# Expert layers with a token-major second layer, the gate folded into the rows, the next rows transposed inside the branch, and an early job of 256 rows

## The chip, the cores and the metric

The kernel runs on one core of a Trainium2 chip. The metric is the device time of one execution, in microseconds. TensorE (PE in the profile, its weight loads PEld) does the matmuls and transposes into PSUM, VectorE (DVE) and ScalarE (ACT) work on PSUM and SBUF, GpSimd (POOL) does some elementwise work and issues the indirect DMAs, SyncE (SP) issues the plain loads.

## The reference

What is computed is a retention layer over 4 batches, 8 heads, 768 positions and 64 channels, and then a mixture of 8 experts in which each of the 3072 tokens goes to one expert:

```python
for t in range(S):
    state = gamma[None, :, None, None] * state + np.einsum('bhd,bhe->bhde', k[:, :, t], v[:, :, t])
    y[:, :, t] = scale * np.einsum('bhd,bhde->bhe', q[:, :, t], state)
...
logits = x @ w_gate
expert_idx = np.argmax(logits, axis=1)
...
gate_w = probs[np.arange(N), expert_idx]
...
    h = np.maximum(x_sorted[lo:hi] @ w1[e], 0.0)
    y_sorted[lo:hi] = h @ w2[e]
...
return (gate_w[:, None] * y).astype(np.float32)
```

Here x is 3072 x 512, w1[e] is 512 x 1024, w2[e] is 1024 x 512, everything in float32.

## The kernel before

**Retention.** The sequence is cut into 6 chunks of 128 positions. A step is one chunk c of one batch b, 24 steps in all, c outer. Step n loads q, k and v (`load`, four steps ahead, on SP), scales and transposes them (`scale_and_transpose`, one step ahead), makes scores and the output row block (`retain`), and a step later the gate logits (`logits`). After the fourth batch of a chunk, `place` finds each token's expert and its rank among that expert's tokens, adds (tile, row) of the tokens to the table `inv` by a matmul (`found`), and writes the chunk's 512 rows of x to DRAM (`x_d`), with the gate weight in an extra column.

**Routing tail.** After the last step, `cnt` counts the tokens of each expert, `arm` holds for each expert the size of its job in steps of 32 tokens, and `index` makes row numbers out of `inv`. The weights of experts 0 and 1 are loaded during retention (steps 12 and 16).

**Experts.** One job for each expert, up to 512 tokens as 4 tiles. `gather` fetches the rows of a job into `xs` (4 indirect DMAs on POOL, issued two experts ahead), `turn` transposes them on TensorE (16 transposes, evicted by DVE into `xTs`). Then a branch over the job's size (`tc.Switch`) runs `layers` on TensorE and ScalarE: layer 1 takes w1 as the stationary operand and the rows as the moving one, layer 2 takes w2 as the stationary operand and the hidden values `hT` as the moving one, so that its output `yp` is channel-major. `put` transposes it back (16 transposes, `try`), DVE multiplies by the gate weight that came along in `xs`, and 4 indirect DMAs scatter the rows to the output. In source order it is: branch of expert e, weights of e+2, `turn(e+1)`, `put(e)`, `gather(e+2)`.

The order on each engine inside retention and between branches comes from the scheduler of the tile framework, within data dependences; engines wait on semaphores, in the order of their own instructions. A matmul in float32 shows as two weight loads and two matmul rows in the trace.

## Time and profile before

| | |
|---|---|
| median of 3 runs | 737.28 us (735.62 to 745.01) |
| the profiled execution, its own time | 741.29 us |
| its span, first to last instruction | 739.5 us |
| PE matmul busy | 602.9 us (82% of the span) |
| PE weight loads busy | 411.1 us (56%) |
| DVE, ACT, POOL busy | 145.0, 91.3, 123.6 us |
| mean granted TensorE clock | 0.874 of full speed (2.4 GHz) |

The span is shorter than the execution's own time by what lies outside the first and last instruction. Busy shares are means over a retention stage, a short routing stage, eight expert stages and a tail, and these have different limits. PE is busy in most of the span, so the time is read from the stretches in which PE is idle or slow and from the work that it does in between.

### The profile page before, as it was taken

What the parts mean: (1) busy time and instruction counts of PE and PEld (TensorE: products, weight loads), DVE (VectorE), ACT (ScalarE), POOL (GpSimd) and SP (SyncE); (2) the same over time, 40 slices, a digit from 0 to 9 for tenths busy, and PEclk for the clock granted to TensorE, in tenths of its full rate; (3) what the DMA queues carried; (4) which work ended last, traced back from release to release, by engine and by line L of the source; (5) the groups of instructions that cost most, each with busy time, mean ns of one, the idle gap of its engine ahead of it and who ended that gap; (6) DMA issues with size and microseconds to landing.
All of it is one profiled execution on the core that took longest, in us unless ns stands there. A gap on an engine that the chain in (4) does not pass through costs nothing. (4 is left out here: it accounts for less than half of the span.)

```text
span 739.5 us, 7581 instructions
## 1 busy us (share of the span) xinstructions
PE 602.9 (82%) x3063; PEld 411.1 (56%) x3063; DVE 145.0 (20%) x330; ACT 91.3 (12%) x175; POOL 123.6 (17%) x159
## 2 busy tenths in 40 slices
PE   6999999998638969966995899499399679869930
PEld 5889899997625535534553454366255345535520
DVE  2554654645420010011002001100200110110020
ACT  2212222122001101100100110010011001001000
POOL 5223222221070010022003100300310220020021
PEclk9979998899858988996997899599699869969975
DMA  9949598931130340332025030403503410020010
GB/s 188 204 113 171 145 300 207 323 73 59 59 87 2 113 135 4 113 114 90 2 113 177 29 113 14 172 18 115 186 21 113 141 61 0 6 78 0 1 45 34
DMA packets 96475, 72.88 MB, mean 99 GB/s; under 512 B 77932, under 2 KB 77932, under 8 KB 96384
## 3 DMA queue, kind: packets, MB, share of 16 engines
q1 hardware_dynamic: 88096, 52.46, 26.2%
q0 software_dynamic: 5120, 12.79, 5.2%
q10 hardware_dynamic: 3168, 6.49, 2.4%
q8 instruction: 48, 0.79, 0.5%
q14 instruction: 43, 0.35, 0.2%
HBM read 61.11 MB, written 14.88 MB: 103 GB/s over the span
## 5 line engine op out<-in xcount | busy, mean ns | idle before, releaser
L395 PE MATMUL hp<-xTs,w1t 128*128 128x416 f32 (+3 forms) x512 | 190.6, 536 | 22.9 <-issue 22.9
L401 PE MATMUL yp<-hT,w2t 128*128 128x416 f32 (+3 forms) x512 | 175.0, 502 | 0.0
L395 PEld LDWEIGHTS hp<-xTs,w1t 128*128 128x128 f32 x512 | 103.6, 204 | 107.6 <-issue 86.8
L401 PEld LDWEIGHTS yp<-hT,w2t 128*128 128x128 f32 x512 | 97.3, 190 | 76.4 <-issue 52.6
L411 DVE TENSOR_SCALAR o<-try,xs 128x512 f32<-128x512 f32 x32 | 22.7, 747 | 356.2 <-PE try L409 348.9
L385 PE MATMUL trs<-ident,xs 128*128 128x128 f32 x128 | 30.7, 389 | 63.8 <-DMA xs<-x_d,at 60.0
L375 POOL DMA_INDIRECT xs<-x_d,at x32 | 32.8, 1026 | 278.0 <-DVE o L411 272.0
L397 ACT ACTIVATE hT<-hp 128x416 f32<-128x416 f32 (+3 forms) x64 | 32.5, 508 | 302.2 <-PE hp L395 302.2
L220 PE MATMUL y<-vs,am 128*128 128x64 f32 x384 | 61.0, 280 | 1.6 <-DVE am L194 0.6
L412 POOL DMA_INDIRECT out_dram<-o,at x32 | 32.1, 1003 | 177.4 <-DVE o L411 105.9
L385 PEld LDWEIGHTS trs<-ident,xs 128*128 128x128 f32 x128 | 20.4, 196 | 73.0 <-issue 59.2
L220 PEld LDWEIGHTS y<-vs,am 128*128 128x128 f32 x384 | 56.2, 207 | 4.0 <-issue 1.8
L386 DVE COPY xTs<-trs 128x512 f32<-128x512 f32 x32 | 21.9, 689 | 113.7 <-PE trs L385 113.7
L194 DVE TENSOR_TENSOR am<-sc,causal 128x512 f32<-128x512 f32 x48 | 31.4, 686 | 52.8 <-PE sc L192 52.8
L216 PE MATMUL y<-stb,qT 128*128 128x128 f32 x160 | 39.5, 331 | 0.0
L192 PE MATMUL sc<-qT,kT 64*128 64x128 f32 x384 | 37.6, 298 | 0.0
L403 ACT COPY yT<-yp 128x416 f32<-128x416 f32 (+3 forms) x32 | 15.9, 496 | 157.7 <-PE yp L401 157.7
L211 POOL COPY stb<-state 64x256 f32<-64x256 f32 x40 | 20.4, 510 | 83.7 <-DVE state L208 82.7
L192 PEld LDWEIGHTS sc<-qT,kT 64*128 64x128 f32 x384 | 29.4, 193 | 3.9 <-issue 2.7
L173 POOL TENSOR_TENSOR vs<-v,dec 128x512 f32<-128x512 f32 x24 | 25.0, 1043 | 36.5 <-PE new L201 26.2
L409 PE MATMUL try<-ident,yT 128*128 128x128 f32 x128 | 25.6, 346 | 4.3 <-DVE xTs L386 2.7
L223 ACT COPY xg<-y 128x512 f32<-128x512 f32 x24 | 14.1, 587 | 110.8 <-PE y L220 110.8
(82 smaller groups left out, 345.1 us busy)
## 6 DMA issues: line engine op xcount, KB each, us to landing
w1t<-in_moe_w_dram SPq DMA_DIRECT2D x8, 2048.0 KB, 7.8
w2t<-in_moe_w_dram SPq DMA_DIRECT2D x8, 2048.0 KB, 12.0
x_d<-xg ACTq DMA_DIRECT2D x6, 1056.0 KB, 4.8
q<-in_q_dram SPq DMA_DIRECT2D x24, 256.0 KB, 4.8
k<-in_k_dram SPq DMA_DIRECT2D x24, 256.0 KB, 4.6
v<-in_v_dram SPq DMA_DIRECT2D x24, 256.0 KB, 4.8
xs<-x_d,at POOLq DMA_INDIRECT x32, 3.5
out_dram<-o,at POOLq DMA_INDIRECT x32, 3.1
```

The lines of the kernel that those rows point to most:

```text
L173: nc.gpsimd.tensor_tensor(out=vs, in0=vt, in1=inner(gk, D), op=ALU.mult)
L192: nc.tensor.matmul(sc[j][:, a, :], lhsT=kT[r, a, :], rhs=qT[r, a, :], start=True, stop=True)
L194: nc.vector.tensor_tensor(out=am[j], in0=sc[j], in1=middle(causal[:, :], HP), op=ALU.mult)
L216: nc.tensor.matmul(y[:, ts(a, P)], lhsT=qT[:, a, :], rhs=stb[b][c % 2][:, a, :], start=True, stop=False, skip_group_check=True)
L220: nc.tensor.matmul(y[:, ts(h, D)], lhsT=am[j][:, a, :], rhs=vs[:, h, :], start=(c == 0), stop=True, skip_group_check=True)
L375: nc.gpsimd.indirect_dma_start(out=xs2[j % 2][:, t, :], out_offset=None, in_=x_d[:, :], in_offset=bass.IndirectOffsetOnAxis(ap=idx[:, t : ...
L385: nc.tensor.transpose(tr[:, dt, :], xs2[j % 2][:, t, ts(dt, P)], ident)
L395: nc.tensor.matmul(hp, lhsT=w1t[:, 0, dt, ts(f, P)], rhs=xT[:, dt, :, 0:m], start=(dt == 0), stop=(dt == DT - 1))
L397: nc.scalar.activation(out=hT[:, f, 0 : TC * m], in_=hp, func=AF.Relu)
L401: nc.tensor.matmul(yp, lhsT=w2t[:, 0, f, ts(d, P)], rhs=hT[:, f, 0 : TC * m], start=(f == 0), stop=(f == FT - 1))
L409: nc.tensor.transpose(tr[:, ts(d, P)], yT2[j % 2][:, d, t, :], ident)
L412: nc.gpsimd.indirect_dma_start(out=out[:, :], out_offset=bass.IndirectOffsetOnAxis(ap=idx[:, t : t + 1], axis=0), in_=o[:, :], in_offset=N ...
```

## The change

- Layer 2 becomes token-major (`layer2`): a tile of 128 tokens of `hT` is the stationary operand and w2, 512 columns wide, the moving one; 8 matmuls accumulate 128 x 512 outputs with the tokens on the partitions, and ScalarE copies them to `o2`. A last tile of 32 or 64 tokens is cut into 4 or 2 column parts, each with its output in other PSUM partitions; a last tile of 96 takes the full 512 columns. The 16 transposes of `put` and the DVE multiplication are gone.
- The gate weight is multiplied into the rows of x by ScalarE in `place`, ahead of the write to `x_d` (the weight is positive, so it passes through the relu). The extra column of `x_d` is gone, and `xs` is free once it is transposed.
- `turn` of the next job stands inside the branch, between the layers, evicted by ScalarE.
- After chunk 4 of 6, the first 256 tokens of expert 0 are indexed and gathered (with padding of the ranks, should there be fewer). Their two layers (`xTa`, `hTa`, `oa`) run on PE right behind the last retention step, with the routing tail interleaved between the blocks of layer 1. Expert 0's later job has only the rest.
- Scatters are declared independent of each other. The last expert scatters inside its branch. Weights of expert 0 are loaded at step 12, those of expert 1 only after retention's tiles are given up; q, k and v have 5 buffers each in place of 6.

The core of the diff:

```diff
-    OV = N // W - 1
-    ROW = DM + 16
+    EARLY = 256
...
-    x_d = dram.tile([N, ROW], F32, tag="x_d", name="x_d")
+    x_d = dram.tile([N, DM], F32, tag="x_d", name="x_d")
...
+    def turn(xs, xT, tiles, evict):
+        for t in tiles:
+            tr = ps("tr", 3, "trs").rearrange("p (a t) -> p a t", a=DT)
+            for dt in range(DT):
+                nc.tensor.transpose(tr[:, dt, :], xs[:, t, ts(dt, P)], ident)
+            evict(out=xT[:, :, ts(t, P)], in_=tr)
+
+    def layer1(n, xT, w1t, hT, f):
+        hp = ps("sc", 2, "hp")[:, 0:n]
+        for dt in range(DT):
+            nc.tensor.matmul(hp, lhsT=w1t[:, 0, dt, ts(f, P)], rhs=xT[:, dt, 0:n], start=(dt == 0),
+                             stop=(dt == DT - 1))
+        nc.scalar.activation(out=hT[:, f, 0:n], in_=hp, func=AF.Relu)
+
+    def layer2(n, hT, w2t, o, t):
+
+        m = min(n - t * P, P)
+        parts = P // m if m in (P // 4, P // 2) else 1
+        y = ps("y", 2, "ye")
+        c = DM // parts
+        for f in range(FT):
+            for j in range(parts):
+                nc.tensor.matmul(y[j * m : j * m + m, 0:c], lhsT=hT[:, f, t * P : t * P + m],
+                                 rhs=w2t[:, 0, f, ts(j, c)], start=(f == 0), stop=(f == FT - 1))
+        for j in range(parts):
+            nc.scalar.copy(out=o[0:m, t, ts(j, c)], in_=y[j * m : j * m + m, 0:c])
+
+    def scatter(o, idx, tiles):
+        for t in tiles:
+            done = nc.gpsimd.indirect_dma_start(
+                out=out[:, :], out_offset=bass.IndirectOffsetOnAxis(ap=idx[:, t : t + 1], axis=0), in_=o[:, t, :],
+                in_offset=None, bounds_check=N - 1, oob_is_err=False)
+
+            tc.declare_no_dep(done.ins, group="scatters", reason="other rows of the output")
+            tc.add_to_no_dep_group("scatters", done.ins)
...
-                t = att.tile([P, H, D], F32, tag=nm, name=nm, bufs=6)
+                t = att.tile([P, H, D], F32, tag=nm, name=nm, bufs=5)
...
+            yield
             for dt in range(DT):
                 nc.tensor.matmul(lg[:, b, :], lhsT=xT[:, dt, :], rhs=wg[:, dt, :], start=(dt == 0), stop=(dt == DT - 1))
+            yield
             if b == B - 1:
-                place(c, lg)
+                yield from place(c, lg)
...
-            gate = xg[c % 2][:, :, DM]
-            den = att.tile([P, B], F32, tag="den", name="den")
-            nc.vector.tensor_reduce(den, ex, axis=AX.X, op=ALU.add)
-            nc.vector.tensor_scalar(out=den, in0=den, scalar1=1e-9, scalar2=None, op0=ALU.add)
-            nc.vector.reciprocal(gate, den)
-            nc.scalar.dma_start(x_d[:, :].rearrange("(b c p) r -> c p b r", c=NC, p=P)[c], xg[c % 2])
...
+            x = xg[c % 2]
+            for b in range(B):
+                nc.scalar.activation(out=x[:, b, :], in_=x[:, b, :], func=AF.Copy, scale=gate[:, b : b + 1])
+            nc.scalar.dma_start(x_d[ts(c, B * P), :].rearrange("(b p) r -> p b r", p=P), x)
+            if c == NC - 2:
...
+                early.append(index(inv[:, :, 0 : EARLY // P], "_e"))
+                gather(xs2[0], early[0][0], range(EARLY // P), (c + 1) * B * P)
...
-            if n in (12, 16):
-                sets.append(weights(len(sets)))
+            if n == 12:
+                wa = weights(first, 0)
...
+        rest = logits(*done)
+        with tc.manual_schedule(engines={mybir.EngineType.PE}):
+            turn(xs2[0], xTa, range(EARLY // P), nc.vector.tensor_copy)
+            for f in range(FT):
+                layer1(EARLY, xTa, wa[0], hTa, f)
+                if f != 4:
+                    next(rest, None)
+            for _ in rest:
+                pass
+            for t in range(EARLY // P):
+                layer2(EARLY, hTa, wa[1], oa, t)
+        scatter(oa, early[0][1], range(EARLY // P))
...
+    o2 = [keep2.tile([P, TC, DM], F32, tag=f"o{i}", name=f"o{i}") for i in range(2)]
+    for t in o2:
+        nc.vector.memset(t, 0.0)
+    sets = [wa, weights(keep2, 1)]
+    cols = [(src_i[:, ts(e, TC)], dst_i[:, ts(e, TC)]) for e in range(E)]
+    HALF = EARLY // P
+
+    gather(xs2[1], cols[0][0], range(HALF, TC))
+    gather(xs2[0], cols[1][0], range(TC))
+    xT = mp.tile([P, DT, W], F32, tag="xTs", name="xTs")
+    turn(xs2[1], xT, range(HALF, TC), nc.vector.tensor_copy)
...
+    for e in range(E):
+        w1t, w2t = sets[e]
+        skip = EARLY if e == 0 else 0
+        arms = MOST - LEAST + 1 - skip // STEP
+        engines = [PE, ACT] + ([POOL] if e == E - 1 else [])
+        which = regs(e, engines)
+        if e + 1 < E:
+            xTn = mp.tile([P, DT, W], F32, tag="xTs", name="xTs")
+        hT = mp.tile([P, FT, W], F32, tag="hT", name="hT", bufs=1)
+        with tc.manual_schedule(engines={PE, ACT}):
+            for a in tc.Switch(which, arms):
+                n = STEP * (LEAST + a)
+                for f in range(FT):
+                    layer1(n, xT[:, :, skip:], w1t, hT, f)
+                if e + 1 < E:
+                    turn(xs2[e % 2], xTn, range(TC), nc.scalar.copy)
+                tiles = -(-n // P)
+                for t in [tiles - 1] + list(range(tiles - 1)):
+                    layer2(n, hT, w2t, o2[e % 2], t)
+                    if e == E - 1:
+                        scatter(o2[e % 2], cols[e][1], [t])
+        if e + 1 < E:
+            tiles = range(TC - HALF) if e == 0 else range(TC)
+            scatter(o2[e % 2], cols[e][1][:, HALF:] if e == 0 else cols[e][1], tiles)
+            xT = xTn
+        if e + 2 < E:
+            gather(xs2[(e + 1) % 2], cols[e + 2][0], range(TC))
+            sets.append(weights(first if e % 2 == 0 else keep2, e + 2))
```

**Where instructions stand, PE, end of retention.** Before, the last gate logits (`trx`, `lg`) are followed by the ranks (`rk`):

```order
L239 MATMUL lg<-wg,xT 128x8 [waits DVE_49]
L239 MATMUL lg<-wg,xT 128x8 x3
L235 MATMUL trx<-ident,xg_116 128x128 [waits Activation_49]
L235 MATMUL trx<-ident,xg_116 128x128 x3
L239 MATMUL lg<-wg,xT 128x8 [waits DVE_49]
L239 MATMUL lg<-wg,xT 128x8 x3
L263 LDWEIGHTS before [waits DVE_49]
L263 MATMUL rk<-ohs,before 128x32 [waits PE_49]
```

After, the early job's transposes (`trs` from `xs_103`) and layer 1 (`hp` from `xTa`) stand among them:

```order
L308 MATMUL lg<-wg,xT 128x8 [waits DVE_49]
L308 MATMUL lg<-wg,xT 128x8 x3
L181 MATMUL trs<-ident,xs_103 128x128 x2
L187 MATMUL hp<-xTa,w1t 128x256 [waits DVE_49]
L187 MATMUL hp<-xTa,w1t 128x256 x3
L303 MATMUL trx<-ident,xg_122 128x128 [waits Activation_49]
L303 MATMUL trx<-ident,xg_122 128x128 x3
L187 MATMUL hp<-xTa,w1t 128x256 x4
L308 MATMUL lg<-wg,xT 128x8 [waits DVE_49]
L308 MATMUL lg<-wg,xT 128x8 x3
L187 MATMUL hp<-xTa,w1t 128x256 [waits Activation_49]
```

The early job's transposes and matmuls now stand between the pieces of the routing tail on PE.

**PE, from the second layer of one expert to the next branch.** Before (the end of an arm of 512 tokens, then the code behind the branch, rows of `turn` and of `put`):

```order
L401 MATMUL yp<-hT,w2t 128x512 [waits Activation_49]
L401 MATMUL yp<-hT,w2t 128x512 x7
L517 UNCONDITIONAL_BRANCH
L385 MATMUL trs<-ident,xs_2248 128x128
L385 MATMUL trs<-ident,xs_2248 128x128 [waits DMASW6_49]
L385 MATMUL trs<-ident,xs_2248 128x128 x3
L385 MATMUL trs<-ident,xs_2248 128x128 [waits DMASW7_49,DVE_49]
L385 MATMUL trs<-ident,xs_2248 128x128 x3
L409 MATMUL try<-ident,yT_2249 128x128 [waits DVE_49] x3
L409 MATMUL try<-ident,yT_2249 128x128 x3
L409 MATMUL try<-ident,yT_2249 128x128 [waits Activation_49]
```

After (an arm of 416 tokens: the end of layer 1, the transposes of the next rows, the last tile of 32 tokens in 4 parts, the first full tile):

```order
L187 MATMUL hp<-xTs,w1t 128x416 x3
L181 MATMUL trs<-ident,xs_104 128x128 [waits DMASW0_49,PE_49]
L181 MATMUL trs<-ident,xs_104 128x128 x3
L181 MATMUL trs<-ident,xs_104 128x128 [waits DMASW1_49,PE_49]
L181 MATMUL trs<-ident,xs_104 128x128 x3
L181 MATMUL trs<-ident,xs_104 128x128 [waits DMASW3_49]
L181 MATMUL trs<-ident,xs_104 128x128 x3
L181 MATMUL trs<-ident,xs_104 128x128 [waits DMASW5_49,Activation_49]
L181 MATMUL trs<-ident,xs_104 128x128 x3
L199 MATMUL ye<-w2t,hT 32x128 [waits DMAHW3_49]
L199 MATMUL ye<-w2t,hT 32x128 x31
L199 MATMUL ye<-w2t,hT 128x512 x8
```

The transposes that wait for gathers and for evictions have moved from behind the branch to between the layers, and the code behind the branch holds none of them.

**POOL, around one expert.** Before, scatters (`out_dram`) and the gathers of the job after next (`xs`) alternate, and a scatter also waits for the scatter before it:

```order
L412 DMA out_dram<-o,at 3072x512 [waits DMASW7_49,DVE_49]
L375 DMA xs_2247<-x_d,at 128x528 [waits DMASW1_49,PE_49]
L375 DMA xs_2247<-x_d,at 128x528 [waits DMASW2_49,DVE_49]
L375 DMA xs_2247<-x_d,at 128x528 [waits DMASW3_49,DVE_49]
L412 DMA out_dram<-o,at 3072x512 [waits DMASW0_49]
L375 DMA xs_2247<-x_d,at 128x528 [waits DMASW5_49,DVE_49]
L412 DMA out_dram<-o,at 3072x512 [waits DMASW4_49]
L412 DMA out_dram<-o,at 3072x512 [waits DMASW6_49]
```

After, the gathers stand behind one scatter and wait for transposes (PE) of the expert before:

```order
L206 DMA out_dram<-o_2400,dst 3072x512 [waits DMASW4_49,Activation_49]
L151 DMA xs_103<-x_d,src 128x512 [waits DMASW5_49,PE_49]
L151 DMA xs_103<-x_d,src 128x512 [waits DMASW6_49,PE_49]
L151 DMA xs_103<-x_d,src 128x512 [waits DMASW7_49,PE_49]
L151 DMA xs_103<-x_d,src 128x512 [waits DMASW0_49,PE_49]
L206 DMA out_dram<-o_2400,dst 3072x512 [waits DMASW1_49,Activation_49]
L590 UNCONDITIONAL_BRANCH
L206 DMA out_dram<-o_2400,dst 3072x512 [waits DMASW2_49]
```

What moved is the gather: all four are issued behind one scatter, with no wait for a scatter's landing.

## Rows read from the trace of the kernel before

**Rows 1.** Stretches: us, then busy of PE, PEld, DVE, ACT, POOL, clock, DMA share, GB/s.

```profile
195.00:224.00 29.00, 8.81 (x46) 5.98 (x45) 10.18 (x36) 0.23 (x1) 15.43 (x12) 0.55 0.31 93
344.00:409.00 65.00, 53.61 (x160) 30.21 (x160) 5.49 (x8) 6.16 (x12) 8.15 (x8) 0.87 0.27 92
```

**Rows 2.** Timeline of PE, experts 1 and 2: start, us, instructions, idle before.

```profile
302.82 22.51 PE L401 MATMUL yp<-hT,w2t 128*128 128x416 f32 x64
...
344.03 24.30 PE L395 MATMUL hp<-xTs,w1t 128*128 128x416 f32 x64 [2.34 <-issue]
368.17 22.51 PE L401 MATMUL yp<-hT,w2t 128*128 128x416 f32 x64
390.51 0.82 PE L409 MATMUL try<-ident,yT 128*128 128x128 f32 x6
```

**Rows 3.** Waits of PE, 224 to 711 us: total, times, longest.

```profile
PE trs L385 <- DMA xs<-x_d,at: 47.3, 14, 7.6
PE hp L395 <- issue: 22.9, 8, 6.2
```

**Rows 4.** Groups by shape, second layer: count, busy us, mean ns.

```profile
L401 PE MATMUL yp<-hT,w2t 128*128 128x416 f32 x256 | 90.0, 512 | 0.0
L401 PE MATMUL yp<-hT,w2t 128*128 128x384 f32 x128 | 41.6, 486 | 0.0
...
L401 PE MATMUL yp<-hT,w2t 128*128 128x448 f32 x64 | 24.2, 539 | 0.0
...
L401 PE MATMUL yp<-hT,w2t 128*128 128x352 f32 x64 | 19.1, 459 | 0.0
```

**Rows 5.** Timeline of PE, end of retention to first rows of expert 0.

```profile
194.03 1.01 PE L239 MATMUL lg<-wg,xT 128*128 128x8 f32 x8
...
196.31 1.06 PE L239 MATMUL lg<-wg,xT 128*128 128x8 f32 x8 [0.78 <-DVE xT L237]
...
213.07 1.09 PE L385 MATMUL trs<-ident,xs 128*128 128x128 f32 x4 [11.20 <-DMA xs<-x_d,at]
```

**Rows 6.** PE's sequencer: loading sizes; jump out of a branch; jump into the next.

```profile
L422 PEldq TENSOR_LOAD <-arm x8: 296/302/845, 201.6 to 207.0; - x8
...
L517 PEldq COMPARE_BRANCH  x1: 3373/3373/3373, 318.9 to 318.9; - x1
...
L517 PEldq COMPARE_BRANCH  x1: 3717/3717/3717, 340.2 to 340.2; - x1
```

**Rows 7.** Stretches after a branch began (columns as in rows 1).

```profile
277.00:279.00 2.00, 1.55 (x3) 0.85 (x4) 0.00 (x0) 0.00 (x0) 0.00 (x0) 0.50 0.16 54
...
285.00:302.00 17.00, 17.00 (x50) 9.31 (x49) 0.00 (x0) 3.11 (x6) 0.00 (x0) 1.00 0.00 0
```

**Rows 8.** Retention: matmuls of one source line (ns), and one run in the timeline.

```profile
L201 PE MATMUL new<-vs,k x320: 221/222/370, 12.9 to 161.9; 128*64 128x64 f32 x160
...
150.63 0.69 PE L201 MATMUL new<-vs,k 128*64 128x64 f32 x16
```

**Rows 9.** DMA issues on the page: count, size, median us to landing.

```profile
w1t<-in_moe_w_dram SPq DMA_DIRECT2D x8, 2048.0 KB, 7.8
...
x_d<-xg ACTq DMA_DIRECT2D x6, 1056.0 KB, 4.8
...
xs<-x_d,at POOLq DMA_INDIRECT x32, 3.5
```

**Rows 10.** Timeline of POOL: two indirect DMAs in a row; the last two scatters.

```profile
327.82 1.01 POOL L375 DMA_INDIRECT xs<-x_d,at  x1 [0.31 <-DVE o L411]
329.13 1.02 POOL L412 DMA_INDIRECT out_dram<-o,at  x1 [0.30 <-issue]
...
725.13 0.98 POOL L412 DMA_INDIRECT out_dram<-o,at  x1 [2.40 <-DMA out_dram<-o,at]
728.56 0.98 POOL L412 DMA_INDIRECT out_dram<-o,at  x1 [2.44 <-DMA out_dram<-o,at]
```

**Rows 11.** Timeline of ACT: one copy of 128 x 512 out of PSUM.

```profile
158.71 0.59 ACT L223 COPY xg<-y 128x512 f32<-128x512 f32 x1 [5.21 <-PE y L220]
```

More of the change, by code (lines that the diff above doesn't have):

```diff
@@ L141, in weights, with gather @@
         return w1t, w2t
+    first = ctx.enter_context(tc.tile_pool(name="first", bufs=1))
+    xs2 = [first.tile([P, TC, DM], F32, tag=f"xs{i}", name=f"xs{i}") for i in range(2)]
+    for t in xs2:
+        nc.gpsimd.memset(t, 0.0)
+    def gather(xs, idx, tiles, rows=N):
+        for t in tiles:
+            nc.gpsimd.indirect_dma_start(
+                out=xs[:, t, :], out_offset=None, in_=x_d[0:rows, :],
+                in_offset=bass.IndirectOffsetOnAxis(ap=idx[:, t : t + 1], axis=0), bounds_check=rows - 1,
+                oob_is_err=False)
@@ new lines @@
+    nc.vector.tensor_scalar(out=arm, in0=arm, scalar1=-float(LEAST), scalar2=None, op0=ALU.add)
+    nc.vector.tensor_scalar(out=arm[:, 0:1], in0=arm[:, 0:1], scalar1=-float(EARLY // STEP), scalar2=0.0, op0=ALU.add,
+                            op1=ALU.max)
+    src_i, dst_i = index(inv, "")
+    PE, ACT, POOL = mybir.EngineType.PE, mybir.EngineType.Activation, mybir.EngineType.Pool
+    mp = ctx.enter_context(tc.tile_pool(name="mp", bufs=2))
+    keep2 = ctx.enter_context(tc.tile_pool(name="keep2", bufs=1))
@@ L416 @@
-    PE, ACT = mybir.EngineType.PE, mybir.EngineType.Activation
-    cols = [at_i[:, ts(e, TC)] for e in range(E)]
-    gather(0, cols[0])
-    gather(1, cols[1])
-    xT = turn(0)
-    for e in range(E):
-        which = {PE: nc.tensor.value_load(arm[0:1, e : e + 1], min_val=0, max_val=ARMS - 1),
-                 ACT: nc.scalar.value_load(arm[0:1, e : e + 1], min_val=0, max_val=ARMS - 1)}
-        for a in tc.Switch(which, ARMS):
-            layers(e, LEAST + STEP * a, xT, *sets[e])
-        if e + 2 < E:
-            sets.append(weights(e + 2))
-        if e + 1 < E:
-            xT = turn(e + 1)
-        put(e, cols[e])
-        if e + 2 < E:
-            gather(e + 2, cols[e + 2])
```

163 lines of the change are left out of this document (72 added, 91 removed).

## The prediction

> **What bounds the kernel now.** I read the stretches first, then PE's timeline over one expert, PE's waits, and the rows of its sequencer. Retention ends near 195 us, with PE busy almost throughout. From 195 to 224 PE is busy for 8.8 of 29 us [rows 1]: it waits for the routing tail and the first gather (11.2 us of that wait alone stand before the first `trs` [rows 5]). Then come eight expert stages. In one of them, 344 to 409, the two layers take 24.3 and 22.5 us [rows 2] of 65 us [rows 1]. The other 18 us are 32 transposes and waits: in all stages together 47.3 us for gathered rows and 22.9 us at the entry of a branch [rows 3]. Nothing but PE works much there (ACT 6.2 us, DVE 5.5 of 65 [rows 1]), so the stage is a chain on PE with holes. After a hole PE restarts at half clock: 0.50 in the first 2 us of a branch, 1.00 eight microseconds later [rows 7]; the first layer costs 24.3 us where the second, of equal size, costs 22.5 [rows 2]. The end is a row of scatters, each issued after the one before has landed [rows 10].
>
> **The change part by part.**
>
> *Price of a matmul.* The shapes of layer 2 give, per matmul row, 0.298 us for 352 columns and 0.378 for 448 (19.1 and 24.2 over 64 [rows 4]), so 0.833 ns a column and 5 ns. By that 512 columns cost 0.432 us, 256 cost 0.218, 128 cost 0.112. The counts in [rows 4] also give the jobs: four of 416 tokens, two of 384, one of 448, one of 352; by the order of the timeline expert 0 has 384.
>
> *Retention.* ScalarE gets 4 multiplications a chunk, at 0.59 us by its copies [rows 11], 14 us in all; it has room, but the next qT copy stands behind them. Fewer q/k/v buffers mean later loads, one weight load less fewer collisions. POOL issues the early gather behind its last retention instruction, so it blocks nobody on its own queue; the early transposes on PE stand in the middle of the last step and wait for it, with the rest of that step's y matmuls behind them. Its chain is a write of x (4.8 us) and a gather (3.5 [rows 9]), against some 10 us of PE work; a tie. I bound the sum of these at 0 and 6 us (a gather and half a write), and take 2.5, nearer to the lower end because the loads are four steps ahead. The 8 early transposes cost 0.9 us: 0.137 each from six in 0.82 [rows 2], less the drain of the last. Logits of step 22 end at 195.0 [rows 5], so layer 1 of the early job starts at **198.4**.
>
> *Early job.* Layer 1 is 64 x 0.218 = 14.0 us, layer 2 of two tiles 32 x 0.432 = 13.8, and the routing tail's own PE work about 2.3, twice its largest piece, `lg` at 1.06 [rows 5]. PE reaches **228.5**. The routing chain beside it (logits, ranks, table, write of x at 4.8 us, gather at 3.5 [rows 9]) I put at 22 us after 198.4, so it is covered; uncovered it would be what PE loses now.
>
> *Into expert 0.* 8 transposes, 0.9 us. Behind them on PE's sequencer stand eight loads of job sizes (201.6 to 207.0 for seven spacings [rows 6], so 6.2 us) and a jump of 3.7 us [rows 6]. How far does the sequencer run ahead? It reached a branch's exit at 318.9 [rows 6], while layer 2 ended at 325.3 [rows 2]: 6.4 us, 18 matmuls of 0.352. With 8 transposes and 10 matmuls still queued (4.3 + 0.9 us of work), 9.9 us of loads and jump leave PE idle for about 4.8 us, and the restart costs 2 (the layers' difference in [rows 2]). Bounds: 0 and 9. Expert 0's rest of 128 tokens starts at **234.2** and takes 7.2 + 2.0 + transposes 2.2 (16 x 0.137 [rows 2]) + 6.9: **252.5**.
>
> *From expert to expert.* PE's queue now ends with full matmuls, 18 x 0.432 = 7.8 us of cover, and the sequencer must jump out (3.4) and in (3.7 [rows 6]), 7.1 and small change. Nothing else stands there, so I take 0.5 us for each of 7 passages, **3.5**; bounds 0 and 25 (below). The weights of expert 1 wait for the early scatters, near 234.5; with 7.8 us to land [rows 9] w1 is there by 243, before 252.5.
>
> *Gathers and scatters.* The gathers of a job are issued behind one scatter, at 1.32 us each [rows 10]; the last lands some 11 us after the stage's start, and its transposes come behind a first layer of 19 us or more. So the 47.3 us [rows 3] go. The next thing that is late is nothing on PE but the jump.
>
> *Experts 1 to 7.* Layer 1: 4 x 22.5 + 24.2 + 19.1 + 20.8 = 154.2, at full clock. Full tiles (the one of 96 tokens costs like a full one): 21 x 16 x 0.432 = 145.1. Transposes between the layers: 6 x 2.2 = 13.2. Last tiles of 32 tokens (four) and of 64 (one): 64 and 32 matmul rows of 128 and 256 columns. If the parts overlap fully, 1.7 and 3.5 us; one after another, 7.2 and 7.0. The nearest row is retention's `new`, whose outputs alternate between partition halves: 16 rows in 0.69 us with 0.22 for the last one's drain [rows 8], 0.029 us each where 64 columns alone would cost 0.058. They overlap by two, so I take near the lower end: 4 x 2.2 + 3.9 = 12.7. Sum **325.2**, and PE ends at 252.5 + 3.5 + 325.2 = **581.2**.
>
> The Trainium skill speaks against this in one place: by "TensorE: Matmul & The Clock Gate", Part 3, what overlaps and what doesn't, a weight load overlaps matmuls in flight only if it goes to another row group, and all parts here use all rows. By that rule and the page's loading time the last tiles would cost 8.6 and 8.5 us, as an estimate, and PE would end some 30 us later. The 0.029 us in [rows 8] speak against it, for parts of 64 columns; no row has parts of 32.
>
> *Tail.* The last copy (0.59 [rows 11]) and its scatter; the order puts two scatters of expert 6 behind it, so the last one is issued 3.5 us after PE's end. From the last issue to the end of the span it was 739.5 - 728.6 = 10.9 us [rows 10], which I keep. Span 581.2 + 14.4 = **595.6**. The profiled execution's own time was 1.8 us over its span and 0.54% over the median of the runs: 597.4 and **594**.
>
> **The rivals.**
>
> *Parts run one after another.* Last tiles cost 7.2 and 7.0: 4 x 5.0 + 3.1 = 23 us more, **617**. For it: 32-token parts are seen nowhere, and 64 pairs in 2 us need a fast sequencer. Against it: [rows 8]. The page's rule above is its harsher form. Chance 0.12.
>
> *The jumps stay visible.* If the two jumps in a row aren't covered, the entry costs what it does now, 2.3 us idle and 1.8 for the restart [rows 2], less 0.5, seven times: 25 us, **619**. For it: cover and need differ by 0.7 us. Chance 0.12.
>
> *The gathers are late as before.* The change would not remove the waits it is said to: PE stands inside the branch, with layer 2 behind it. 47.3 us [rows 3] and seven restarts of 1.8: **654**. Against it: 19 us of layer 1 where before there was nothing in between. Chance 0.03.
>
> *Slower than before.* The one way I see is the clock: PE granted half of it over much of the expert stage, because transposes and short matmuls stand among the long ones. All of the 368 us of matmul work at 1.2 GHz would give 960; above 740 it gets when 39% of it (144 us) runs so. For it: 0.50 after every hole [rows 7]. Against it: 1.00 within every layer, and fewer holes. Chance 0.02, with some 0.01 for ending near 740.
>
> **How the numbers follow.** The forecast, 594, has 0.70. Its own range is 580 (all lower bounds but one) to 606. The two rivals at 617 and 619 are taken into the range with what lies around them, so 580 to 626; beyond it lie the late gathers, the clock, and some of each end. A measurement of this kernel can tell about 2% from no change, 15 us; every case but the clock is far past that: faster 0.97, same 0.01, slower 0.02.
>
> **What would show it.** Right: PE nearly without idle from 198 to the end of the last expert, except for about 5 us ahead of expert 0; no wait of `trs` for `xs`; granted clock near 1.00 in the expert stages; last tiles near 2 us. Wrong: a `ye` row of 32 tokens at 0.11 us per matmul, idle time of `hp` put down to issue at every branch, or a `trs` wait inside a branch. What would spoil it most is a hole that recurs in each expert, since each microsecond of it counts seven times and brings a restart.

## The result and the profile after

| | before | after |
|---|---|---|
| median of 4 runs each, interleaved | 736.45 us (729.4 to 745.01) | 637.06 us (627.53 to 643.04) |
| ratio | | 0.857 (0.844 to 0.871) |
| profiled execution, own time and span | 741.29 and 739.5 us | 627.53 and 625.7 us |
| PE matmul busy | 602.9 us | 563.8 us |
| mean granted clock | 0.874 | 0.947 |

Faster by 14%, but 43 us over the forecast and above its range. Executions of one kernel differ by 2 to 4% here; the ratio's interval comes from undisturbed runs.

The stretches of the profile after, in the columns of [rows 1]: the end of retention with the early job, and the stage of experts 1 to 7.

```profile
193.00:226.00 33.00, 31.95 (x140) 21.88 (x139) 7.17 (x40) 7.38 (x16) 9.43 (x10) 1.00 0.27 87
...
245.00:611.00 366.00, 336.53 (x1168) 173.65 (x1168) 0.00 (x0) 56.83 (x119) 41.79 (x43) 0.95 0.28 95
```

The 29 us at the end of retention in which PE had 8.8 us of work [rows 1] are full. Experts 1 to 7 still leave PE idle for 29.5 of 366 us. PE's waits tell where; they answer to [rows 3]:

```profile
PE hp L187 <- ACT hT L189: 27.8, 7, 5.3
PE tr L246 <- DVE qs L240: 7.0, 2, 5.4
PE rk L334 <- DVE ohs L330: 2.1, 4, 1.2
PE hp L187 <- issue: 2.0, 1, 2.0
PE hp L187 <- DVE xTs L182: 1.7, 1, 1.7
```

The 47.3 us for gathered rows are gone, and so are the 22.9 us put down to issue, but for 2.0 at the entry of expert 1. In their place stands a wait that the kernel before did not have: layer 1 for ScalarE, seven times, 27.8 us. The timeline of all engines, without PE's weight loads, at the passage from expert 1 to expert 2 (start, us, instructions, idle before):

```profile
298.64 5.75 PE L187 MATMUL hp<-xTs,w1t 128*128 128x416 f32 x16
298.84 0.37 SPq L141 DMA_DIRECT2D w2t<-in_moe_w_dram  x1
298.84 0.59 ACT L202 COPY o<-ye 128x512 f32<-128x512 f32 x1 [6.28 <-PE ye L199]
299.71 1.03 POOL L206 DMA_INDIRECT out_dram<-o,dst  x1 [6.50 <-ACT o L202]
...
307.84 0.93 ACT L189 ACTIVATE hT<-hp 128x416 f32<-128x416 f32 x2 [8.41 <-issue]
308.41 1.06 PE L187 MATMUL hp<-xTs,w1t 128*128 128x416 f32 x1 [4.02 <-ACT hT L189]
```

PE itself passes here without a gap: its layer 2 ends and layer 1 begins at 298.64. It does 16 matmuls, which fill the two PSUM buffers of `hp`, and stops at 304.4, because ScalarE, which must empty them, is on its way from one branch into the next. ScalarE copied the last tile of expert 1 at 298.84 and does its first instruction of expert 2 at 307.84, 8.4 us after the end of that copy. In that moment SyncE issues 2 MB of `w2`, whose buffer has just come free. What the stop costs besides shows in the stretches behind it (columns of [rows 1]):

```profile
304.40:308.40 4.00, 0.00 (x0) 0.00 (x0) 0.00 (x0) 0.56 (x2) 0.00 (x0) 0.79 0.99 381
308.40:311.00 2.60, 2.59 (x4) 1.51 (x5) 0.00 (x0) 0.37 (x1) 0.00 (x0) 0.50 0.25 95
311.00:315.00 4.00, 4.00 (x9) 1.95 (x8) 0.00 (x0) 0.52 (x1) 0.00 (x0) 0.68 0.00 0
315.00:327.00 12.00, 12.00 (x36) 6.55 (x35) 0.00 (x0) 2.07 (x4) 0.00 (x0) 1.00 0.00 0
```

PE idle for 4 us, the DMA engines 99% busy, then half clock as in [rows 7]: the other 48 rows of that layer 1 take 19.57 us where expert 7, with a stop of 0.74 us, has 17.03.

```profile
308.41 19.57 PE L187 MATMUL hp<-xTs,w1t 128*128 128x416 f32 x48 [4.02 <-ACT hT L189]
...
570.11 17.03 PE L187 MATMUL hp<-xTs,w1t 128*128 128x416 f32 x48 [0.74 <-ACT hT L189]
587.07 22.75 PE L199 MATMUL ye<-w2t,hT 128*32 128x128 f32 x112
```

Into expert 7 nothing is loaded. The last row answers to [rows 2] for layer 2: three tiles of 6.87 us and a last tile of 32 tokens in 2.1.

### The profile page after: what moved, and what is told of

Its sections match the earlier page's. It is cut to its first block, busy times and chain, and to the rows that moved or that the text cites. A ratio compares the mean times of both kernels' runs of the same rounds, so it can differ in the third digit from the quotient of the medians.

```text
span 625.7 us, 7784 instructions
## 1 busy us (share of the span) xinstructions
PE 563.8 (90%) x3160; PEld 371.6 (59%) x3160; DVE 108.5 (17%) x291; ACT 123.8 (20%) x245; POOL 118.8 (19%) x156
## 4 chain that ended last, share of the span: by engine, by line
issue 56%; PE 28%; POOL 8%; DVE 4%; DMA 1%; POOLq 1%; SPq 0%; DVEq 0%
PE y L288 7%; POOL out_dram L206 4%; PE sc L260 4%; POOL xs L151 4%; PE tr L246 4%; PE y L284 4%; PE lg L308 3%; PE new L269 2%; PE hp L187 2%; PE trx L303 2%; DVE am L262 1%; DMA q<-in_q_dram 1%; DVE xT L305 0%; DVE state L276 0%; SPq L232 0%
## 5 line engine op out<-in xcount | busy, mean ns | idle before, releaser
L187 PE MATMUL hp<-xTs,w1t 128*128 128x416 f32 (+4 forms) x512 | 177.9, 509 | 31.5 <-ACT hT L189 27.8
L199 PE MATMUL ye<-w2t,hT 128*128 128x512 f32 (+3 forms) x640 | 164.0, 455 | 0.0
L199 PEld LDWEIGHTS ye<-w2t,hT 128*128 128x128 f32 (+3 forms) x640 | 74.8, 155 | 84.2 <-issue 83.2
L206 POOL DMA_INDIRECT out_dram<-o,dst x30 | 29.8, 995 | 294.3 <-ACT o L202 236.7
L189 ACT ACTIVATE hT<-hp 128x416 f32<-128x416 f32 (+4 forms) x64 | 30.0, 480 | 178.5 <-PE hp L187 123.7
L151 POOL DMA_INDIRECT xs<-x_d,src x30 | 30.3, 1009 | 72.6 <-PE ye L199 35.5
L284 PEld LDWEIGHTS y<-stb,qT 128*128 128x128 f32 x160 | 25.6, 202 | 1.3
L246 PE MATMUL tr<-ident,qs 128*128 128x128 f32 x96 | 18.5, 318 | 7.0 <-DVE qs L240 7.0
L308 PE MATMUL lg<-wg,xT 128*128 128x8 f32 x192 | 24.5, 254 | 0.3
L308 PEld LDWEIGHTS lg<-wg,xT 128*128 128x128 f32 x192 | 23.4, 192 | 1.7 <-DVE xT L305 1.2
```

Of the source, the lines that this page charges most:

```text
L151: nc.gpsimd.indirect_dma_start(out=xs[:, t, :], out_offset=None, in_=x_d[0:rows, :], in_offset=bass.IndirectOffsetOnAxis(ap=idx[:, t : t + ...
L187: nc.tensor.matmul(hp, lhsT=w1t[:, 0, dt, ts(f, P)], rhs=xT[:, dt, 0:n], start=(dt == 0), stop=(dt == DT - 1))
L189: nc.scalar.activation(out=hT[:, f, 0:n], in_=hp, func=AF.Relu)
L199: nc.tensor.matmul(y[j * m : j * m + m, 0:c], lhsT=hT[:, f, t * P : t * P + m], rhs=w2t[:, 0, f, ts(j, c)], start=(f == 0), stop=(f == FT ...
L206: done = nc.gpsimd.indirect_dma_start(out=out[:, :], out_offset=bass.IndirectOffsetOnAxis(ap=idx[:, t : t + 1], axis=0), in_=o[:, t, :], i ...
L246: nc.tensor.transpose(tr[:, a, :], src[:, 2 * a : 2 * a + 2, :].rearrange("p h d -> p (h d)"), ident)
```

## The experiments

Two theories stood at first. Contention: ScalarE's way into a branch is long because of the 2 MB on their way. Rival: it is long by itself. Executions differ most in retention, so the table sets two times of each profile apart: when the early job's layer 1 starts (predicted 198.4 us, with this kernel's retention code in all rows but the last three), and the part from there to the end of the span (predicted 595.6 - 198.4 = 397.2).

| run | median, us (lowest to highest) | early layer 1 starts, us | part behind it, us | stops of PE for ScalarE at the entries of branches, us in all |
|---|---|---|---|---|
| the changed kernel | 637.06 (627.5 to 643.0) | 195.3 | 430.4 | 27.8 |
| f0_same | 639.83 (631.0 to 653.2) | 210.0 | 431.4 | 28.0 |
| e1_no_late_weights | 612.42 (603.3 to 617.3) | 211.8 | 396.0 | 6.5 |
| e2_w2_early | 635.06 (626.0 to 636.8) | 205.2 | 428.3 | 25.1 |
| e3_third_bank | 608.31 (600.2 to 627.1) | 221.1 | 404.2 | 11.8 |
| e4_both | 606.26 (594.9 to 622.1) | 209.5 | 399.7 | 9.0 |
| f1_dve_evicts | 600.85 (590.5 to 611.7) | 201.3 | 387.5 | none |
| f2_w2_pinned | 608.42 (601.7 to 614.1) | 207.1 | 402.4 | 10.2 |
| f3_one_part | 662.26 (661.3 to 676.4) | 205.5 | 454.0 | 29.9 |
| h1_turn_at_entry | 670.63 (667.6 to 676.5) | 207.3 | 467.4 | 57.2 + 3.4 |
| h3_half_load | 611.12 (602.8 to 614.1) | 204.2 | 402.3 | 11.6 |
| r0_dve_again | 597.40 (594.6 to 610.4) | 207.6 | 388.7 | none |
| r1_xs_zero_dve | 590.17 (585.4 to 595.8) | 198.6 | 387.7 | none |
| r2_no_gate | 590.70 (589.3 to 603.8) | 192.5 | 395.0 | none |
| r3_split_load | 597.69 (591.4 to 603.4) | 209.6 | 388.2 | none |

**e1: no weight loads in the expert stages** (experts 2 to 7 use the weights of experts 0 and 1; the loads are left out).

```diff
-            sets.append(weights(first if e % 2 == 0 else keep2, e + 2))
+            sets.append(sets[e])
```

> Leaves out the weight loads of experts 2 to 7; they compute with the weights of experts 0 and 1. Theory A (ScalarE's code for the next branch is fetched through the same DMA engines as w2 of the expert after next, which is issued at the branch's exit): every passage becomes like the one into expert 7, where nothing is loaded: PE's wait for hT 0.7 us in place of 3.6 to 5.3, 27.8 in all falls to about 5, the restarts at half clock mostly go, span 625.7 falls to about 592. Theory B (ScalarE's two jumps in a row are long in themselves): the waits stay near 27 us and the span near 625.

The time lies between, but the profile decides: the stops fall from 27.8 to 6.5 us, ScalarE comes into the experts 2 to 7 after 5.1 to 5.3 us, and the part behind the early job falls from 430.4 to 396.0 us. What is missing to 592 lies in retention, where the early job began 16.5 us later than in the first profile. Contention, then, for the stops.

**e2 and e4: a third buffer for `w2`; e3: a third PSUM buffer for `hp`** (the bank of `lg`, for the third slice of layer 1; e4 has both edits).

```diff
+            nc.sync.dma_start(w1n, w1v[:, ds(e + 2, 1), :, :])
+            nc.sync.dma_start(ring[(e + 2) % 3], w2v[:, ds(e + 2, 1), :, :])
...
-        hp = ps("sc", 2, "hp")[:, 0:n]
+        hp = (ps("lg", 1, "hp") if spare and f == 2 else ps("sc", 2, "hp"))[:, 0:n]
```

> Gives w2 a third buffer, so that w2 of expert e+2 is loaded right behind w1 of e+2, during the second layer of expert e, and not at the exit of its branch. All loads stay. Theory A: near the run without late loads, waits of hp for hT 5 to 10 us in all, span 592 to 600. Theory B: waits near 27 us, span near 625.

> Loads stay as they are; the third block of layer 1 in a branch writes to the PSUM bank that the gate logits used, so PE can run three blocks (8.4 us at 416 columns) before it needs ScalarE, not two (5.6). Both theories: the wait shrinks by one block of 2.4 to 3.0 us, to 1 to 2.5 us a passage, some 10 us in all; span about 605 by the waits alone, down to 595 if the shorter holes also spare the restarts.

> Early w2 and the third bank together. Theory A: no wait of hp for hT is left except into expert 1, span 586 to 592. Theory B: like the third bank alone, about 600 to 605.

e2 gained nothing, as the rival said, but it was not the test it was meant to be: SyncE's queue got the load of `w2` one expert further ahead, and so it again waited for a buffer freed at the passage (issued at 311.83, when layer 1 of expert 2 began at 311.64). One passage of it tells something, the one into expert 6, for which nothing was left to load. Expert 5 and expert 6 in PE's timeline of e2:

```profile
482.32 20.04 PE L187 MATMUL hp<-xTs,w1t 128*128 128x416 f32 x48 [4.26 <-ACT hT L189]
...
533.15 15.75 PE L187 MATMUL hp<-xTs,w1t 128*128 128x384 f32 x48 [1.18 <-ACT hT L189]
```

In the changed kernel expert 6 waited 5.08 us there. e3 holds whatever the reason for ScalarE's delay: 2.8 us more of cover (work that PE can do before it needs ScalarE) take 16 us of stops. e4 came out much like e3 alone, since its load of `w2` was as late as that of e2.

**f0: the changed kernel again; f1: VectorE empties layer 2 inside the branches.**

```diff
-            nc.scalar.copy(out=o[0:m, t, ts(j, c)], in_=y[j * m : j * m + m, 0:c])
+            evict(out=o[0:m, t, ts(j, c)], in_=y[j * m : j * m + m, 0:c])
...
-        engines = [PE, ACT] + ([POOL] if e == E - 1 else [])
+        engines = [PE, ACT, DVE] + ([POOL] if e == E - 1 else [])
...
+                    layer2(n, hT, w2t, o2[e % 2], t, nc.vector.tensor_copy)
```

> The changed kernel itself once more, beside the next three on one chip. Two theories on the 33 us by which its profiled execution is over the predicted span: all of it lies behind the early job (its part from the first row of the early layer 1 to the end of the span was 625.7 - 195.3 = 430.4 us, where 397.2 was predicted), or retention has a share too that the one execution did not show. In the four profiles of the first experiments the early job began at 205 to 221 us, with the same retention code, where it began at 195.3 in the first profile of this kernel. The first theory expects it near 195 to 200 again, the second between 203 and 221. The part behind it should be 425 to 435 by both. Time 630 to 645.

> VectorE goes into the branches and takes the PSUM copies of layer 2 from ScalarE, whose last instructions in a branch are then the copies of the transposed rows, some 20 us before PE leaves it. The weight loads stay where they are. Theory: what PE waits for behind its first 16 rows of a branch is ScalarE alone, which jumps in too late; then the stop behind the 16th row is gone in all seven passages, the waits of hp for hT fall from 27.8 us to under 3, the restarts at half clock go with them, and the part from the early layer 1 to the end is 395 to 402 us; the time some 30 us under the changed kernel's on the same chip. Rival: something else is behind the stop (the jump of PE itself, the arrival of weights), so the waits only change their name; the part stays over 420. A cost of its own can come at the next entry of VectorE, which leaves late in ScalarE's place, but nothing waits for it until layer 2, 20 us later.

f0 came as its second theory has it: its early job began at 210.0 us, so retention has a share in the miss that the first profile did not show, and the part behind it is the same 431 us. f1 came as its theory has it, and by more: the stops are gone, and the part behind the early job is 387.5 us, under the 395 to 402 expected. The same passage in the timeline of f1, again without weight loads:

```profile
299.31 5.05 PE L187 MATMUL hp<-xTs,w1t 128*128 128x416 f32 x14
299.50 0.37 SPq L141 DMA_DIRECT2D w2t<-in_moe_w_dram  x1
299.51 0.69 DVE L202 COPY o<-ye 128x512 f32<-128x512 f32 x1 [6.17 <-PE ye L199]
...
302.36 0.52 ACT L189 ACTIVATE hT<-hp 128x416 f32<-128x416 f32 x1 [24.81 <-PE hp L187]
```

The load is issued as before, but ScalarE left 20 us earlier and now waits for PE. Layer 1 is one unbroken row of 64 matmuls in each of the experts 1 to 7, 22.5 us for 416 columns, and PE goes from 252.44 to 572.6 without a stop, at full clock (columns of [rows 1]):

```profile
252.44:572.60 320.16, 320.16 (x1168) 167.51 (x1168) 19.23 (x38) 40.45 (x80) 43.12 (x43) 1.00 0.31 107
```

**f2: `w2` really early** (e2 with SyncE's order pinned).

```diff
+            with tc.manual_schedule(engines={mybir.EngineType.SP}):
+                nc.sync.dma_start(w1n, w1v[:, ds(e + 2, 1), :, :])
+                nc.sync.dma_start(ring[(e + 2) % 3], w2v[:, ds(e + 2, 1), :, :])
```

> The second experiment as it was meant: a third buffer for w2, and SyncE's order pinned, so that w2 of expert e+2 is loaded right behind w1 during layer 2 of expert e and has landed some 8 us before the passage. Without the pin the order put it back at the passage. Theory of contention: ScalarE takes 8.4 to 9.1 us to the first instruction of a branch because 2 MB are on their way in that moment; in the second experiment the one passage of those with no load had 1.2 us of wait where the others had 4.0 to 5.4. Then all seven have about 1, the waits of hp for hT fall from 27.8 to 5 to 8 us, the part from the early layer 1 to the end is 396 to 403 us, the time some 28 us under the changed kernel's. Rival: the two jumps of ScalarE are as long without the load; then 4 to 5 us of wait in each passage stay, and the time is within 8 us of the changed kernel's.

Contention: with nothing on its way ScalarE takes 5.2 us instead of 8.4, with the same two jumps, and PE stops for 0.8. The passage from expert 1 to expert 2 in f2's timeline, without weight loads:

```profile
312.89 5.75 PE L187 MATMUL hp<-xTs,w1t 128*128 128x416 f32 x16
313.09 0.59 ACT L202 COPY o<-ye 128x512 f32<-128x512 f32 x1 [6.28 <-PE ye L199]
...
318.89 0.93 ACT L189 ACTIVATE hT<-hp 128x416 f32<-128x416 f32 x2 [5.22 <-PE hp L187]
319.46 2.71 PE L187 MATMUL hp<-xTs,w1t 128*128 128x416 f32 x7 [0.83 <-ACT hT L189]
```

The passage into expert 1, where weights are still on their way, keeps 4.4 of the 10.2 us.

ScalarE's sequencer shows which part of the way is longer. These are its two jumps, out of the branch of expert 1 and into that of expert 2, and the first instruction behind the second jump (a prefetch hint), in the changed kernel and then in f2:

```profile
L590 ACTq COMPARE_BRANCH  x2: 38/42/47, 298.9 to 301.4; - x2
L479 ACTq BRANCH_PREFETCH_HINT  x1: 31/31/31, 307.7 to 307.7; - x1
```

```profile
L596 ACTq COMPARE_BRANCH  x2: 38/42/47, 313.1 to 315.7; - x2
L481 ACTq BRANCH_PREFETCH_HINT  x1: 31/31/31, 318.8 to 318.8; - x1
```

The way out takes as long in both, 2.4 us from the first jump to the next instruction. The way in takes 6.3 us with the load and 3.1 without. The trace also has the time of each DMA packet. The page lists q14 as a queue of instructions, and 0.9 us behind the first jump a packet of it starts in both. Behind the second jump the first packet of q14 starts after 3.8 us in the changed kernel and after 0.7 us in f2, and ScalarE goes on 2.5 and 2.4 us later. Over the passages into the experts 2 to 6 it starts 2.7 to 4.4 us behind the second jump in the changed kernel, and 0.4 to 0.7 us in e1 and f2. So ScalarE's instructions come late while the weights are under way; in the passage shown the rest of the way is as long as without them.

**h3: half of `w2` (1 MB) at the passage.**

```diff
+                nc.sync.dma_start(ring[(e + 2) % 3][:, :, HF:, :], w2v[:, ds(e + 2, 1), HF:, :])
+                    nc.sync.dma_start(ring[e % 3][:, :, 0:HF, :], w2v[:, ds(e + 3, 1), 0:HF, :])
```

> As the version with three w2 buffers and SyncE's order pinned, except that the first half of w2 (1 MB) is loaded at the passage and the second half with w1 during the layer 2 before. It asks for the dose. With 2 MB at the passage ScalarE's first instruction comes 8.4 to 9.1 us after its last, with nothing 5.1 to 5.3 or hidden, and hp waits 4.0 to 5.3 against 0.3 to 1.6 us. If ScalarE's instructions come in as a part of the DMA traffic that is held up by the load for as long as it lasts, 1 MB (4 to 6 us of it) holds them up about half as long: waits of 2 to 3.5 us, 620 to 628 us in all. If any load in that moment delays it in full, because what it needs comes in the first microseconds, the waits stay 4 to 5 us and the time 632 to 642. If only the tail of a long load hurts, they are near 1 and the time 608 as with nothing at the passage.

Stops of 0.6 to 1.7 us behind expert 1, as if nothing were loaded. It does not give the dose: half a buffer is free after half of the last tile, so the load was issued at 305.39, 3.4 us before ScalarE's last copy. By its packets it had landed 0.6 us before ScalarE's second jump at this passage, and 0.4 to 1.7 us before it at the next three. That a delay grows with what is still on its way stays an inference.

**h1: the transposes back at the entry of their own job.**

```diff
+                if e:
+                    turn(xs2[(e - 1) % 2], xT, range(TC), nc.scalar.copy)
                 for f in range(FT):
                     layer1(n, xT[:, :, skip:], w1t, hT, f)
-                if e + 1 < E:
-                    turn(xs2[e % 2], xTn, range(TC), nc.scalar.copy)
```

> The transposes go back to the job they belong to: each branch from expert 1 on begins with the 16 transposes of its own rows, copied by ScalarE, where the changed kernel has the next job's between the layers. The rows have landed long before by either order. Theory of cover: ScalarE's first instruction of a branch comes 8 to 9 us after its last one of the branch before, and PE's queue reaches as far as the PSUM buffers that ScalarE must empty; with layer 1 first that is 5.8 us of matmuls (two buffers), with the transposes first three buffers, 1.5 us. So the stop per passage grows from 4 to 5 us by 4.3 to some 9, the last copy before layer 1 (about 1 us) comes on top, and seven times 5 to 5.5 us make the time 35 to 39 us longer than the changed kernel's: 672 to 680. Rival: the stop hangs on something that ScalarE's buffers don't set (weights, PE's own jump), then only the copies ahead of layer 1 are added, 1 to 2 us a passage, 645 to 655.

The theory of cover holds: 36 us over f0 in the part behind the early job (467.4 and 431.4), where 35 to 39 were expected; 31 by the medians and 34 by the ratios to the kernel before (0.904 and 0.858, times 741 us), which hold retention's scatter too. PE's waits in h1: the same late ScalarE, with 1.5 us of work ahead of it instead of 5.8.

```profile
PE trs L181 <- ACT xTs L182: 57.2, 7, 9.8
...
PE hp L187 <- ACT xTs L182: 3.4, 5, 0.7
```

**f3: last tiles in one part.**

```diff
-        parts = P // m if m in (P // 4, P // 2) else 1
+        parts = 1
```

> A last tile of 32 or 64 tokens is no longer cut into column parts: each matmul row has 512 columns and writes only 32 or 64 partitions. If the parts overlap on PE as the trace of the changed kernel shows (64 rows of 32 by 128 in 2.0 us), this costs 16 rows of 0.432 us each time: four times 4.9 us and 3.4 us for the tile of 64, 23 us more than the changed kernel on the same chip, about 660. If something else than PE set the time there, less than 8 us. One copy in place of four or two leaves ScalarE free earlier, but this tile comes first in layer 2, so nothing follows from that at the passage.

22.6 us over f0 in the part behind the early job (454.0 and 431.4), where 23 were expected; 22.4 by the medians and 29 by the ratios to the kernel before (0.896 and 0.858). Layer 2 of expert 7 takes 5.1 us more than in the changed kernel:

```profile
615.64 27.85 PE L199 MATMUL ye<-w2t,hT 128*32 128x512 f32 x64
```

**h0: retention of the kernel before, once more.**

> The kernel before once more, for its retention alone. Its first profile has the logits of step 22 done at 195.0 us, with the granted clock at half in about four of the 6-us stretches between 18 and 195 us; five profiles of the changed kernel's retention code ended later, at 201 to 221 us, and one at 195.3. If the half-clock stretches vary from execution to execution whatever the kernel, this one ends somewhere between 195 and 215 us too, most likely later than the first. If the changed retention (the multiplications by the gate, five buffers instead of six, the early index) brings them, it ends at 193 to 198 us again. One execution can speak for the first only by ending late; an end near 195 would leave it open.

The logits of step 22 end at 193.7 us here (192.71 + 1.01), 195.0 in the first profile. So retention before is steady, as far as two profiles go, and the changed one is not: in twelve profiles of that code the early layer 1 starts at 195.3 to 221.1 us, median 207.2. PE's groups of instructions stand in the same order in all twelve, so the order alone does not set the start. Between 18 and 195 us PE is busy as long in f0 as in the kernel before, but gets through fewer instructions, at a lower clock (columns of [rows 1]; the kernel before in this run, then f0). The first profile of the changed kernel, which began the early job at 195.3, has 1691 matmul rows there at a clock of 0.94, as the kernel before.

```profile
18.00:195.00 177.00, 171.94 (x1689) 158.49 (x1687) 90.89 (x229) 38.49 (x72) 41.33 (x59) 0.93 0.66 167
```

```profile
18.00:195.00 177.00, 171.58 (x1582) 158.47 (x1583) 87.95 (x234) 49.88 (x89) 41.55 (x61) 0.87 0.58 139
```

**r0 to r3: a search for what brings it.** All three edits stand on f1, which is r0; r2 and r3 contain r1. r2 leaves out the multiplication of x by the gate.

```diff
     for t in xs2:
-        nc.gpsimd.memset(t, 0.0)
+        nc.vector.memset(t, 0.0)
...
-            for b in range(B):
-                nc.scalar.activation(out=x[:, b, :], in_=x[:, b, :], func=AF.Copy, scale=gate[:, b : b + 1])
...
+            if n == 16:
+                w2a = first.tile([P, 1, FT, DM], F32, tag="w2t", name="w2t")
```

> The version in which VectorE empties layer 2 inside the branches, once more, as the measure for the next three on its chip. Nothing is changed; 590 to 612 us as before, its early layer 1 starting between 200 and 212 us, where the prediction of the changed kernel had 198.4.

> The version in which VectorE empties layer 2, with one more edit: the two buffers for gathered rows are set to zero by VectorE instead of GpSimd. In the changed kernel these 3.5 us stand first on GpSimd, so that the first product vs is done 2.9 us later than in the kernel before (10.1 instead of 7.2 us) and PE's first instructions are ordered otherwise: it stops for 0.9 us at its third group and reaches full clock at 18 to 24 us; the logits of step 0 came at 28 us in most profiles, 24.9 in the kernel before. With the edit PE's order at the start is that of the kernel before. Theory that the opening costs what retention lost: the early layer 1 starts 3 to 5 us sooner than in the version without the edit, near 200, and the time falls by as much. Rival: the half-clock stretches later in retention make up the loss by themselves and come wherever they come; then the start moves, the early layer 1 by less than 2 us.

> As the last, and the multiplication of x by the gate is left out (the output lacks the gate). These are four instructions of ScalarE in a row for each chunk, 2.56 us, ahead of the copies of qT and xg. In the changed kernel the half-clock stretches of retention come behind the place in each chunk where the ranks are made. Theory: the four instructions delay the copies that PE needs there, so without them the stretches behind 78 us shrink to the two of the kernel before and the early layer 1 starts at 193 to 197. Rival: PE waits there for VectorE (0.2 to 0.6 us for am and for total), not for ScalarE; then the start is that of the last version, within 2 us.

> As the version with VectorE's zeros, with expert 0's weights loaded in two pieces, w1 at step 12 and w2 at step 16, where the changed kernel loads 4 MB at step 12. The longest half-clock stretch of most profiles (about 120 to 138 us) stands in that load, with the DMA engines at 1.0 to 1.2 of their time. Theory: q, k and v come late behind 4 MB, PE runs short and the clock falls; then the stretch shortens by half or more and the early layer 1 starts 4 to 8 us sooner. Rival: the stretch follows from the stop for the ranks, as the others do; then it stays, within 2 us.

r1 is 7.2 us faster than r0 by the medians, but the intervals of the ratios to the kernel before overlap (0.792 to 0.802, and 0.800 to 0.811 for r0). Its early job starts at 198.6 against 207.6 in r0, but f1, the same kernel as r0, had 201.3, so these profiles do not show an effect of the zeros. The zeros in f0's and in r1's timeline of POOL:

```profile
2.87 3.54 POOL L147 MEMSET xs<- 128x2048 f32 x2
6.36 3.75 POOL L400 MEMSET stb<- 128x512 f32 x8
10.08 2.03 POOL L241 TENSOR_TENSOR vs<-v,dec 128x512 f32<-128x512 f32 x2
```

```profile
2.87 3.75 POOL L400 MEMSET stb<- 128x512 f32 x8
7.12 1.04 POOL L241 TENSOR_TENSOR vs<-v,dec 128x512 f32<-128x512 f32 x1 [0.50 <-DMA v<-in_v_dram]
```

If the zeros matter, it is not by the path that I expected: the first product `vs` is 2.9 us later with them, but the logits of step 0 came at 23.8 us in r0 and 24.8 in r1, so the opening itself was no later. What r1 also changes is the order on PE in the first steps, again that of the kernel before, and a few places behind. In these two profiles r1 has the higher clock in the stretch from 18 to 195 us; r0, then r1:

```profile
18.00:195.00 177.00, 171.68 (x1593) 157.56 (x1594) 87.27 (x232) 50.63 (x91) 41.19 (x61) 0.86 0.59 143
```

```profile
18.00:195.00 177.00, 170.48 (x1669) 156.10 (x1667) 92.22 (x241) 50.49 (x91) 43.48 (x61) 0.93 0.60 146
```

r2 starts the early job 6 us sooner still, so the multiplications may cost up to that, but one profile is not enough; it gave the gain back in one 8.7-us wait of PE ahead of expert 0. r3 did what neither theory said: its early job starts 11 us later than r1's, with the 48 us from 18 us on at a clock of 0.72 where r1 has 0.89, although it has r1's zeros too. With 26 us between profiles of unchanged code, none of the three edits is shown to be the cause, nor shown not to be. r1 has the lowest median of the versions with the whole computation: 590.17 us, 0.930 of the changed kernel by the ratios of both to the kernel before. Most of that is f1's edit, which alone (r0) comes to 0.939.

## Why the prediction was wrong, and where it was right

**The step that failed** is "From expert to expert": "Nothing else stands there, so I take 0.5 us for each of 7 passages". It counted the cover of PE's queue against the jumps of PE's own sequencer. That arithmetic holds for six passages, in which f1 has no gap. Into expert 1 PE's own jump shows, 2.0 us in the changed kernel and 1.1 in f1, since only one tile of expert 0 stands ahead of it. But a branch is entered by each engine for itself, and ScalarE's way in was not priced. In the kernel before it was as long: 8.7 to 9.7 us from its jump out of a branch to its first instruction in the next, in the six passages with a load on its way. There it lay beside the 18 us between the two experts. The change gave ScalarE the last copies of a branch, and loads 2 MB as it leaves: 8.4 to 9.1 us, against 5.8 us of matmuls that fit into two PSUM buffers.

From the end of expert 0 (243.5 us) to PE's end (609.8) it took 366.3 us, where f1 does the same work in 320.2. So the passages cost 46 us in place of 3.5: 27.8 for ScalarE, 2.0 for PE's own jump, and a rest of 16, most of it in rows at less than full clock behind the stops (14.4 in layer 1 of experts 1 to 6, against the same rows in f2). The part behind the early job is only 430.4 - 397.2 = 33.2 us over the forecast, because other terms were too high: the early job and expert 0 took 48.2 us in place of 54.1, the work of experts 1 to 7 5.0 us less; the tail took 1.5 more. The forecast of that part was thus helped by 9 us of errors the other way. The rival "the jumps stay visible" named the place, by the wrong engine, and 25 of the 43 us.

**A term that was mis-sized** is retention, 2.5 us with bounds of 0 and 6. The early job began 207.2 - 198.4 = 8.8 us later than forecast in the median of twelve profiles, and 3.1 us sooner in the profiled execution of the changed kernel. The list had ScalarE's multiplications and the buffers, but not the zeros for the gathered rows, which the change moves ahead of the first product on GpSimd; nor did it have the clock, which differs between executions of this code. Which of these makes the 8.8 us is not shown. The two together make 595.6 + 33.2 + 8.8 = 637.6 us of span, 639 with 1.8 us around it; medians of 637 and 640 were measured. r1 came to 590 where 594 was forecast, but that is partly luck: it has f1's edit and the errors named above.

**Right, by their own steps:**
- No wait for gathered rows inside a branch; the 47.3 us went.
- The early job covers the routing chain: PE waits 1.7 us ahead of expert 0 (for copies of the transposed rows), where 4.8 us for the jump, and a restart, were put.
- Work of experts 1 to 7: 325.2 predicted, 320.2 in f1, 1.5% less.
- Column parts overlap: 2.1 us for 64 rows, 3.9 for the tile of 64 tokens (2.2 and 3.9 predicted); undone, 22.6 us (23 predicted for "parts run one after another"). By the prediction's estimate from the rule in the Trainium skill, "TensorE: Matmul & The Clock Gate", Part 3, on what overlaps, these tiles would have taken 8.6 and 8.5 us; the measurement decides against it here.
- Tail: 15.9 us behind PE's end, 14.4 predicted.
- Slower than before: in the expert stages the clock fell only behind holes. It was 1.00 throughout in f1, which has none there. In retention that does not hold: in r0 it fell from 1.00 to 0.50 at 30 us, with PE busy for 33.0 of the 33 us from 15 to 48.

**Open:** why the clock in retention falls oftener in some executions of the same code than in others, and what part the change has in it; and at what point on their way ScalarE's instructions wait for the weights.

## What to carry to other kernels

When a change joins PE's work across a jump, price the way into the next branch for every engine that PE will need there, up to the PSUM buffer at which PE must wait for it; then give the last instructions of a branch to an engine that the next one needs late. Look at what comes free in that moment, since its load starts there, and read from the queue's order whether a further buffer really moves a load. Where profiles of unchanged code lie 26 us apart in one stage, take that stage and the rest apart, as in the table above, and take several profiles before an edit is credited with a few microseconds of it.

## What the runs showed of the hardware

- ScalarE took 5.1 to 5.4 us from its last instruction in one branch to the first of the next with no load on its way (e1 and f2, into experts 2 to 7), 8.4 to 9.1 with 2 MB of `w2` on their way (the changed kernel, into experts 2 to 6). The difference lies behind the second jump, in the wait for a packet of the instruction queue q14: its first packet starts 0.4 to 0.7 us behind the jump without the load (e1 and f2, into experts 2 to 6), 2.7 to 4.4 with it (the changed kernel). The packet itself is no longer, 0.3 us with and without the load in the passage from expert 1 to expert 2. That they share DMA engines with the weights fits this, but no run shows it. The page of the changed kernel lists these queues:

```profile
q8 instruction: 48, 0.79, 0.6%
q14 instruction: 44, 0.36, 0.2%
```

- A stop of 4.0 us on PE was followed by a granted clock of 0.50 (1.2 GHz) up to 311 us, 0.68 from 311 to 315, and 1.00 (2.4 GHz) from there; stops of 0.3 to 1.7 us (f2, h3) cost no more than themselves: 17.03 us for the 48 rows behind them.
- Four column parts of 32 x 128 run side by side: 64 matmul rows in 2.1 us, 0.03 us each.
